# One core, attention, routed experts and a gated FFN: a spare score bank, weight splits moved to the first expert pass, and a later hand-over to the fast product

## The chip, the cores and the metric

The kernel runs on one core of a Trainium2 chip. The metric is the device time of one execution in microseconds (us). It is told as the median of the runs shown, and a profiled execution is taken beside them.

## The reference, cut to what matters

Three stages follow each other on 2304 tokens of width 512: banded causal attention, a top-2 choice among eight experts, and a gated feed-forward layer.

```python
mask = (rel >= 0) & (rel < 64)                        # attention: B=4, H=8, S=576, D=64
scores = np.where(mask, scale * q @ k.T, -1e9)
attn = softmax(scores); x = attn @ v                  # -> x [2304, 512]
logits = x @ w_gate + log1p(exp(x @ w_noise)) * noise # 8 experts, the two best are kept
for e in range(8):                                    # rows that chose e, weighted
    out[mask] += top2_w[mask, k, None] * (np.maximum(x[mask] @ w1[e], 0) @ w2[e])
h = out @ w_in                                        # 512 -> 2048
g = np.where(h >= 1, h, np.where(h <= -1, 0.0, (h + 1) ** 2 / 4))
return (g @ w_out).astype(np.float32)
```

`w_in` and `w_out` are float64 in the inputs. The kernel computes products of fp32 numbers by splitting each operand into a high part (fp32r, a copy on ScalarE) and a low part (the rest, a subtraction on VectorE), and it sums hi*hi, lo*hi and hi*lo.

## The kernel before

**Order.** The scheduler keeps the order that the program writes (`manual_schedule`), so each engine runs its instructions in that order and waits at each one for what it needs. An instruction that waits holds up all that is written behind it on the same engine.

**Attention** runs in 37 steps `step(u)`. A *unit* `u` is one score tile of 128 partitions by four heads' 128 columns. `A(i)` makes the scores of units `2i` and `2i+1` on TensorE: four mask matmuls (L352) and 32 score matmuls (L361). `top(u)` takes the maximum on VectorE (L368, L370), `soft(u)` the exponential on ScalarE (L377, four instructions), `C(u)` transposes the probabilities (L384) and copies them (L386), and `Dm(u)` multiplies with the values into the two PSUM banks `OB` (L398) and scales (L403 to L406). Scores rotate over three banks, `Sb[u % 3]`, so unit 3 uses the bank of unit 0. Before step 0 stand nine matmuls on zeros, `A(0)`, `top` and `soft` of units 0 and 1, and four more matmuls on zeros (`warm`, into `OB[:, 1, :]`). The loads of SP's queue go out in the order q and k of block 0, v of tile 0, q and k of block 1, v of tile 1.

Two other jobs ride on the steps. The routing of tokens to experts (`route`, `place`) uses VectorE for most of its small operations. The weights of the first expert come in eight chunks of 128 x 1024; of the first seven (`EW`) the high part is made by `split_w` on ScalarE and the low part by `rest_w` on VectorE (L149), one half chunk in a step; those of the sixth and seventh chunk (c = 5, 6) fall in steps 25, 26, 29 and 30.

**Experts.** `seq` is a list of (pass, chunk). Pass 0 (`0a`) takes three row blocks of expert 0, pass 1 (`0b`) the other two, pass 2 expert `e1` in six blocks, and so on to `7a` and `7b`. For a chunk `mm1` makes the hidden rows (L885), ScalarE and VectorE make their high and low parts (L893, L896) and `mm2` adds them up in one PSUM bank per block (L949). `do_mm1` runs one chunk ahead. In pass 0 `tail()`, a generator, is advanced twice per chunk; it finishes the routing (`finish_ids`, `count`). In the last chunks of a pass the rows of the next one are fetched and transposed (`xpose`: TensorE L756, ScalarE L759, VectorE L760). All six blocks of `e1` are turned in bank 7 (`TR`), and blocks 4 and 5 both at chunk 6 of pass 1 (`turn_at`).

**The gated layer.** The first group of two blocks (`g0`) runs `plain(p)` for p = 0 to 7, with two hidden chunks f = 0, 1 in each. `act_gate` makes the gate of one of them: two operations on ScalarE (L903, L904), two on VectorE (L905, L906), then the high part (ScalarE, L909) and the low part (VectorE, L910). `plain(p+1)` is written ahead of the `mm2` of p. The four groups behind it, of four blocks each, use a product with seven multiplications (`wino`, L1163). Its inputs are made out of the expert results in DRAM: the loads `prep_gather` (POOL's queue for the first such group, `g1`), `mix_two` (ScalarE L1019, VectorE L1021), the transposes `xturn` (TensorE, L1221), `xcopy` (ScalarE, L1227), the sums `xsums` (VectorE, L1240) and the splits `split_two` (ScalarE L1250, VectorE L1252). For `g1` these stand inside the plain items of `g0`. `FILL[(p, f)]` lists what `act_gate` of `plain(p)`, f does between its two VectorE operations and the high part: first the ScalarE half of each entry, and behind the low part the VectorE half. What stands under `(p, j)` is done in the seventh parts j of the `mm2` of p:

```python
FILL.update({(2, 1): [later(mix_two, units[g1], b) for b in (0, 1)],
             (3, 0): [later(mix_two, units[g1], b) for b in (2, 3)], ...
elif p == 2:
    if j in (0, 1, 5, 6):
        xturn(ui + 1, j if j < 2 else j - 3)
```

`FILL[(2, 1)]` is issued with `plain(2)`, one item ahead, so the turns of blocks 0 and 1 stand right behind `plain(3)`, at the head of the `mm2` of item 2.

Of the kernel before, what the change touches and what calls it, by code (L numbers as in the profile page):

```python
# [31 lines left out]
NB = 5  # L32
# [25 lines left out]
def fused_kernel(ctx, tc, qT, kT, v, wg, noise, wcat, out, wd=None):  # L58
# [195 lines left out]
    load_qk(0)  # L254
    load_v(0)
    load_qk(1)
# [86 lines left out]

    def A(i):
        j = i // 2
        qo, ko = (i % 2) * P, (i % 2) * P
        sb = [Sb[(2 * i + k) % 3] for k in range(2)]
        for k in range(2):
            r = slice(64 * k, 64 * k + 64)
            for c in range(2):  # L350
                m = masks[c][int((2 * i + c) % 9 == 0)]
                nc.tensor.matmul(sb[k][64 * c:64 * c + 64, :], lhsT=id64[r, :],  # L352
                                 rhs=m[r].unsqueeze(1).to_broadcast([64, 4, P]), start=True, stop=False)
        for g in range(4):
            for c in range(2):
                for k in range(2):
                    r = slice(64 * k, 64 * k + 64)
                    keys = k_t[j][r, g, ko + 64 * c:ko + 64 * c + P]
                    if c == 0:
                        keys = keys.rearrange("p (s n) -> p s n", s=2)[:, ::-1, :]  # L360
                    nc.tensor.matmul(sb[k][64 * c:64 * c + 64, g * P:g * P + P],  # L361
                                     lhsT=q_t[j][r, g, qo + 64 * c:qo + 64 * c + 64],
                                     rhs=keys, start=False, stop=(g == 3))

    def top(u):
        mx = wk.tile([P, 4], F32, tag="mx", name=f"mx{u}", bufs=3)
        nb = wk.tile([P, 4], F32, tag="nb", name=f"nb{u}", bufs=3)
        nc.vector.tensor_reduce(out=mx, in_=Sb[u % 3].rearrange("p (g n) -> p g n", g=4), axis=AX.X, op=ALU.max)  # L368

        (nc.vector if u < 4 else nc.gpsimd).tensor_scalar(out=nb, in0=mx, scalar1=-0.125, scalar2=None, op0=ALU.mult)  # L370
        mxs[u] = nb

    def soft(u):
        sb, nb = Sb[u % 3], mxs.pop(u)
        p = wk.tile([P, 4, P], F32, tag="p", name=f"p{u}", bufs=4)
        for g in range(4):
            nc.scalar.activation(p[:, g, :], sb[:, g * P:g * P + P], AF.Exp, bias=nb[:, g:g + 1], scale=0.125)  # L377
        pr[u] = p
# [294 lines left out]
    def step(u):  # L673
# [35 lines left out]
        for c in range(EW):  # L709
            for h in range(2):  # L710
                if u == L0 + LS * c + 3 + h:
                    split_w(c, h)
                if u == L0 + LS * c + 4 + h:
                    rest_w(c, slice(512 * h, 512 * h + 512))
            if u == L0 + LS * c + 4 and EW <= c + 2 < NF:
                load_raw(c + 2)
# [76 lines left out]
    def tail():  # L793
# [6 lines left out]
        count()  # L800
# [10 lines left out]
    def count():  # L811
# [25 lines left out]
                                in1=tf[:, 0:R].unsqueeze(2).to_broadcast([P, R, E]), op=ALU.is_equal)  # L837
        for a, src in enumerate((src_i, dst_i)):
# [59 lines left out]

    def act_gate(ps, hh, hl, w):
# [3 lines left out]
        nc.scalar.activation(r, ps, AF.Relu, bias=1.0)  # L903
        nc.scalar.activation(m, r, AF.Copy, scale=0.5)  # L904
        nc.vector.scalar_tensor_tensor(out=r, in0=m, scalar=1.0, in1=r, op0=ALU.min, op1=ALU.subtract)  # L905
        nc.vector.scalar_tensor_tensor(out=r, in0=m, scalar=1.0, in1=r, op0=ALU.min, op1=ALU.mult)  # L906
        for x in parts_of:
            next(x)
        nc.scalar.activation(hh, r, AF.Copy, scale=-1.0)  # L909
        nc.vector.scalar_tensor_tensor(out=hl, in0=r, scalar=-1.0, in1=hh.bitcast(F32), op0=ALU.mult, op1=ALU.subtract)  # L910
# [206 lines left out]
    def plain(ui, p):  # L1117
        w = wi[p % WS]
        for f in range(2):
# [6 lines left out]
            mm1_of(key, n, units[ui]["T"], act_gate, units[ui]["m1"], part(0), part(1))  # L1126
        load_in(p + WS)
# [130 lines left out]
    def copy_two(ui, b):  # L1258
        xcopy(ui, b)
        yield  # L1260

    def sums_two(ui, part):
        yield
        xsums(ui, part)

# [15 lines left out]
    for s in range(len(seq)):  # L1281
# [41 lines left out]
        def ahead_xpose():  # L1323
            for x, b, w in ahead:
                if f == (turn_at[b] if ui == WIDE - 1 else w + 2):
                    prep_xpose(x, b, bank[0] if ui == WIDE else TR)
# [24 lines left out]
        do_mm2(s, ahead_xpose)  # L1351
        for _ in range(SPLITS[ui][f] if ui in SPLITS else int(0 < ui < U7A)):
# [22 lines left out]
        if ui == U7B and f:  # L1375
# [6 lines left out]
          {(5, 3): (6,)})  # L1382
    g1 = FIRST2 + 1

    def later(fn, *a):
        return lambda: fn(*a)
    FILL.update({(2, 1): [later(mix_two, units[g1], b) for b in (0, 1)],
                 (3, 0): [later(mix_two, units[g1], b) for b in (2, 3)],
                 (4, 0): [later(split_two, g1, 0), later(split_two, g1, 1)],
                 (4, 1): [later(sums_two, g1, (0, 1))],  # L1390
                 (5, 0): [later(sums_two, g1, (2, 3))],
                 (5, 1): [later(split_two, g1, j) for j in (2, 3)],
                 (6, 0): [later(split_two, g1, j) for j in (4, 5)]})
    ndone = 1
    for q, (ui, p) in enumerate(items):
# [22 lines left out]
        for j in range(7):  # L1418
            if nxt:
# [12 lines left out]
                elif p == 2:  # L1432
                    if j in (0, 1, 5, 6):
                        xturn(ui + 1, j if j < 2 else j - 3)
                    for b in {3: (0, 1), 6: (2, 3)}.get(j, ()):
                        xcopy(ui + 1, b)
                for x in AT[late].get((p, j), ()):
# [40 lines left out]
```

## Time and profile before

| | |
|---|---|
| median of three runs | 971.39 us (968.99 to 973.98) |
| the profiled execution | 971.69 us, of which the span from first to last instruction is 969.9 |
| busy in the span | TensorE 944.0 us (97%), weight loads 834.8, VectorE 661.6, ScalarE 447.5, GpSimd 220.2 |
| mean granted TensorE clock | 0.994 of full speed |

TensorE is busy nearly always, so the time is that of its work, of its waits (some 26 us) and of stretches at the lower clock. A share of busy time over the whole span says little about one stage: VectorE is busy 68% of the span, and in one stretch of attention all the time.

### The profile page before, as it was taken

Reading aid. Unit: us, or ns where it says so; the run is one execution under the profiler, and the core shown is the slowest. Engines: PE = TensorE matmul, PEld = TensorE weight load, DVE = VectorE, ACT = ScalarE, POOL = GpSimd, SP = SyncE. Lnnn points to the kernel's source line nnn. Section 1 sums busy time; section 2 is a strip of 40 time slices with the busy share of each in tenths; the row PEclk is TensorE's granted clock in tenths of the full one; section 3 lists DMA queues with packets and bytes.
Section 4 is the critical chain, followed back from the end, with each engine's and each line's share of the span. In section 5 each row is a group of like instructions: output and inputs, shape, how many; then the busy total and the mean of one; then the engine's idle time right before and its main releaser. Section 6 shows DMA issues by size and latency. Waiting matters only on the chain. (4 is left out here: it accounts for less than half of the span.)

```text
span 969.9 us, 18052 instructions
## 1 busy us (share of the span) xinstructions
PE 944.0 (97%) x6781; PEld 834.8 (86%) x6781; DVE 661.6 (68%) x1388; ACT 447.5 (46%) x920; POOL 220.2 (23%) x273
## 2 busy tenths in 40 slices
PE   8998999999999999999999997999999999999998
PEld 6886878988898989889888886898999889889897
DVE  4689565378997968889543365766766677577664
ACT  6897324345555555555432355334334333443222
POOL 3221113132634354254402130013002201300000
PEclk9999999999999999999999998999999999999999
DMA  8874125445878878757727574684576558546531
GB/s 249 296 266 144 56 97 187 178 167 192 291 257 290 260 244 278 254 196 251 252 82 239 178 234 159 200 298 155 174 249 230 173 174 295 165 161 214 189 106 44
DMA packets 91274, 196.95 MB, mean 203 GB/s; under 512 B 7320, under 2 KB 18072, under 8 KB 91184
## 3 DMA queue, kind: packets, MB, share of 16 engines
q1 hardware_dynamic: 83152, 171.68, 53.6%
q0 software_dynamic: 6736, 21.86, 6.3%
q10 hardware_dynamic: 1296, 2.23, 0.6%
q8 instruction: 54, 0.88, 0.4%
q14 instruction: 36, 0.29, 0.1%
HBM read 155.45 MB, written 40.29 MB: 202 GB/s over the span
## 5 line engine op out<-in xcount | busy, mean ns | idle before, releaser
L949 PE MATMUL bank<-wo,hall 128*128 128x512 f32 x864 | 239.5, 396 | 0.0
L949 PE MATMUL bank<-w,hall 128*128 128x512 f32 (+3 forms) x944 | 236.0, 398 | 1.4 <-DVE hall L896 1.3
L949 PEld LDWEIGHTS bank<-w,hall 128*128 128x128 f32 (+3 forms) x944 | 168.4, 184 | 37.0 <-DVE hall L896 1.7
L949 PEld LDWEIGHTS bank<-wo,hall 128*128 128x128 f32 x864 | 147.8, 190 | 17.5
L893 ACT ACTIVATE hall<-bank 128x288 fp32r<-128x288 f32 (+6 forms) x128 | 54.0, 422 | 223.3 <-PE bank L885 204.1
L885 PE MATMUL bank<-xhie,w 128*128 128x288 f32 (+4 forms) x768 | 123.0, 302 | 1.6 <-DVE hall L896 1.5
L885 PEld LDWEIGHTS bank<-xhie,w 128*128 128x128 f32 x768 | 113.9, 189 | 9.1 <-DVE hall L896 3.4
L896 DVE SCALAR_TENSOR_TENSOR hall<-bank,hall 128x288 fp32r<-128x288 f32 (+7 forms) x168 | 59.8, 391 | 87.2 <-ACT hall L893 78.5
L149 DVE TENSOR_TENSOR w<-raw,w 128x1024 fp32r<-128x1024 f32 (+1 forms) x71 | 82.4, 1160 | 24.4 <-ACT w L158 20.5
L1163 PEld LDWEIGHTS bank<-xb,wi 128*128 128x128 f32 x576 | 80.4, 188 | 11.5 <-DVE wg L1148 1.2
L1187 ACT ACTIVATE hall<-cg 128x512 fp32r<-128x512 f32 x64 | 40.3, 629 | 100.5 <-DVE cg L1185 100.5
L1163 PE MATMUL bank<-xb,wi 128*128 128x256 f32 x576 | 84.8, 283 | 1.8 <-ACT r L903 0.8
L1163 PEld LDWEIGHTS bank<-xc,wi 128*128 128x128 f32 x480 | 67.2, 188 | 7.6 <-DVE wg L1148 0.6
L1030 POOL TENSOR_TENSOR y<-y,y 128x512 f32<-128x512 f32 x14 | 19.1, 1363 | 227.2 <-ACT y L1029 227.2
L1163 PE MATMUL bank<-xc,wi 128*128 128x256 f32 x480 | 70.2, 281 | 0.2
L158 ACT ACTIVATE w<-raw 128x1024 fp32r<-128x1024 f32 (+1 forms) x71 | 69.3, 976 | 0.0
L885 PE MATMUL bank<-xloe,w 128*128 128x288 f32 (+4 forms) x384 | 69.0, 301 | 0.0
L204 POOL TENSOR_TENSOR td<-rawd 128x512 f32<-128x512 f32 x32 | 33.3, 1039 | 140.7 <-DVE rawd L202 78.2
L1181 ACT ACTIVATE mg<-cg 128x512 f32<-128x512 f32 x64 | 40.1, 626 | 47.1 <-DVE cg L1153 45.4
L1182 DVE SCALAR_TENSOR_TENSOR cg<-mg,cg 128x512 f32<-128x512 f32 x64 | 47.0, 734 | 18.8 <-ACT mg L1181 18.8
L885 PEld LDWEIGHTS bank<-xloe,w 128*128 128x128 f32 x384 | 58.0, 188 | 0.0
L1191 DVE SCALAR_TENSOR_TENSOR hall<-cg,hall 128x512 fp32r<-128x512 f32 x64 | 45.9, 718 | 9.1 <-ACT hall L1187 8.7
(279 smaller groups left out, 1443.5 us busy)
## 6 DMA issues: line engine op xcount, KB each, us to landing
wi<-w1o SPq DMA_DIRECT2D x56, 1024.0 KB
raw<-wcat SPq DMA_DIRECT2D x64, 512.0 KB
rawd<-wd SPq DMA_DIRECT2D x32, 512.0 KB
w1o<-so SPq DMA_DIRECT2D x64, 256.0 KB
y<-y_dram SPq DMA_DIRECT2D x28, 256.0 KB
vE<-v SPq DMA_DIRECT2D x18, 260.0 KB
x_dram<-x SPq DMA_DIRECT2D x18, 256.0 KB
k<-kT SPq DMA_DIRECT2D x8, 512.0 KB
```

What stands on the lines that cost most here:

```text
L149: nc.vector.tensor_tensor(out=w[:, 1, c], in0=t[:, c], in1=w[:, 0, c].bitcast(F32), op=ALU.subtract)
L158: nc.scalar.activation(w[:, 0, c], t[:, c], AF.Copy)
L204: nc.gpsimd.tensor_tensor(out=t, in0=hf, in1=lf, op=ALU.add)
L885: nc.tensor.matmul(ps, lhsT=l[k], rhs=r[:, k, s:s + w], start=(c == 0), stop=(c == len(prods) - 1))
L893: nc.scalar.activation(hh, ps, AF.Relu)
L896: nc.vector.scalar_tensor_tensor(out=t, in0=ps[:, c], scalar=0.0, in1=hh[:, c].bitcast(F32), op0=ALU.max, op1=ALU.subtract)
L949: nc.tensor.matmul(M2[b][0:w], lhsT=h2[:, o:o + w], rhs=r[n], start=(first and a == 0), stop=(last and a == end))
L1163: nc.tensor.matmul(ps, lhsT=w[:, l, k * P:k * P + P], rhs=r[:, m, k, :], start=(c == 0), stop=(c == len(prods) - 1))
L1181: nc.scalar.activation(st["m"], c, AF.Relu, scale=0.5)
L1182: nc.vector.scalar_tensor_tensor(out=c, in0=st["m"], scalar=1.0, in1=c, op0=ALU.min, op1=ALU.subtract)
L1187: nc.scalar.activation(h2[:, 0:T], c, AF.Copy, scale=-1.0)
L1191: nc.vector.scalar_tensor_tensor(out=h2[:, T:2 * T], in0=c, scalar=-1.0, in1=h2[:, 0:T].bitcast(F32), op0=ALU.mult, op1=ALU.subtract)
```

## The change

1. The load of q and k of block 1 goes out ahead of v of tile 0.
2. Unit 3 takes its scores in `OB[:, 0, :]` and not in the bank of unit 0.
3. The low parts of chunks 5 and 6 are left out of the steps and made, each as one operation of 1024 columns, behind the `mm2` of chunks 0 and 2 of pass 0.
4. `count` gets a `yield` ahead of its last four operations.
5. The gate's last two operations (L909, L910) are held back to the next call of `act_gate`, behind its first one; `close_gate` does the last pair.
6. The sixth block of `e1` is transposed into bank 4, the others in bank 7 as before.
7. For `g1` the mixing, turning, copying, sums and splits move to later items.

```diff
     load_qk(0)
+    load_qk(1)
     load_v(0)
-    load_qk(1)
     load_v(1)
...
+    def score(u):
+        return OB[:, 0, :] if u == 3 else Sb[u % 3]
...
-        sb = [Sb[(2 * i + k) % 3] for k in range(2)]
+        sb = [score(2 * i + k) for k in range(2)]
...
-                if u == L0 + LS * c + 4 + h:
+                if u == L0 + LS * c + 4 + h and c < EW - 2:
                     rest_w(c, slice(512 * h, 512 * h + 512))
...
-        count()
+        yield from count()
...
+    held_gate = []
+    def close_gate():
+        for r, hh, hl in held_gate:
+            nc.scalar.activation(hh, r, AF.Copy, scale=-1.0)
+            nc.vector.scalar_tensor_tensor(out=hl, in0=r, scalar=-1.0, in1=hh.bitcast(F32), op0=ALU.mult,
+                                           op1=ALU.subtract)
+        held_gate.clear()
...
         nc.scalar.activation(r, ps, AF.Relu, bias=1.0)
+        close_gate()
         nc.scalar.activation(m, r, AF.Copy, scale=0.5)
...
+        held_gate.append((r, hh, hl))
         for x in parts_of:
             next(x)
-        nc.scalar.activation(hh, r, AF.Copy, scale=-1.0)
-        nc.vector.scalar_tensor_tensor(out=hl, in0=r, scalar=-1.0, in1=hh.bitcast(F32), op0=ALU.mult, op1=ALU.subtract)
...
+        if p == NPR - 1:
+            close_gate()
...
-                    prep_xpose(x, b, bank[0] if ui == WIDE else TR)
+                    prep_xpose(x, b, bank[0] if ui == WIDE else bank[4] if ui == WIDE - 1 and b == NB else TR)
...
         do_mm2(s, ahead_xpose)
+        if s in (0, 2):
+            rest_w(EW - 2 + s // 2, slice(0, 1024))
...
+    TURN, COPY = {(3, 0): (0,), (3, 1): (1,), (3, 6): (2,), (4, 0): (3,)}, {(3, 3): (0, 1), (4, 2): (2, 3)}
...
-    FILL.update({(2, 1): [later(mix_two, units[g1], b) for b in (0, 1)],
-                 (3, 0): [later(mix_two, units[g1], b) for b in (2, 3)],
-                 (4, 0): [later(split_two, g1, 0), later(split_two, g1, 1)],
-                 (4, 1): [later(sums_two, g1, (0, 1))],
-                 (5, 0): [later(sums_two, g1, (2, 3))],
-                 (5, 1): [later(split_two, g1, j) for j in (2, 3)],
-                 (6, 0): [later(split_two, g1, j) for j in (4, 5)]})
+    FILL.update({(3, 0): [later(mix_two, units[g1], 0)],
+                 (3, 1): [later(mix_two, units[g1], 1)],
+                 (4, 0): [later(mix_two, units[g1], b) for b in (2, 3)],
+                 (5, 0): [later(split_two, g1, j) for j in (0, 1)],
+                 (6, 0): [later(split_two, g1, j) for j in (2, 3)],
+                 (6, 1): [later(split_two, g1, j) for j in (4, 5)],
+                 (7, 0): [later(split_two, g1, 6)]})
...
+                else:
+                    for b in TURN.get((p, j), ()):
+                        xturn(ui + 1, b)
+                    for b in COPY.get((p, j), ()):
                         xcopy(ui + 1, b)
+                    if p == 4 and j > 4:
+                        xsums(ui + 1, (0, 1) if j == 5 else (2, 3))
```

## Rows read from the trace of the kernel before

**Rows 1.** Windows: stretch; busy us (count) of PE, PEld, DVE, ACT, POOL; clock; DMA share; GB/s.

```profile
30.00:40.00 10.00, 10.00 (x185) 8.96 (x188) 6.49 (x15) 9.00 (x27) 2.66 (x8) 1.00 0.81 268
...
70.00:80.00 10.00, 9.44 (x155) 8.08 (x151) 9.86 (x38) 8.78 (x27) 2.11 (x6) 1.00 0.88 297
```

**Rows 2.** Waits of TensorE over the span: who for whom, us in total, times, longest.

```profile
PE bank L1221 <- DVE y L1021: 5.5, 1, 5.5
PE bank L352 <- ACT p L377: 1.9, 2, 1.0
PE bank L756 <- DVE xloe L760: 1.8, 2, 1.5
...
PE bank L1163 <- ACT r L903: 0.8, 1, 0.8
PE bank L1163 <- ACT sg L1144: 0.6, 1, 0.6
```

**Rows 3.** Timeline of the start: start, duration, instruction [idle before, releaser].

```profile
7.94 2.17 ACT L377 ACTIVATE p<-bank,nb 128x128 f32<-128x128 f32 x8 [5.86 <-DVE nb L370]
9.13 0.41 PE L352 MATMUL bank<-mask,id 64*64 64x512 bf16 x2 [0.95 <-ACT p L377]
10.97 0.40 POOL L114 COPY k<-k 128x256 f32<-128x256 f32 x1 [1.42 <-DMA k<-kT]
11.03 0.60 ACT L386 ACTIVATE pt<-bank 128x512 f32<-128x512 f32 x1 [0.92 <-PE bank L384]
12.71 0.40 PE L352 MATMUL bank<-mask,id 64*64 64x512 bf16 x2 [0.94 <-ACT p L377]
```

**Rows 4.** The low parts in attention: group over 69 to 95 us, then VectorE's timeline.

```profile
L149 DVE TENSOR_TENSOR w<-raw,w x4: 681/682/689, 70.6 to 88.1; 128x512 fp32r<-128x512 f32 x4
...
70.64 0.69 DVE L149 TENSOR_TENSOR w<-raw,w 128x512 fp32r<-128x512 f32 x1
71.24 0.69 DVE L368 TENSOR_REDUCE mx<-bank 128x4 f32<-128x512 f32 x1
```

**Rows 5.** Windows of attention's late steps, same columns as rows 1.

```profile
69.00:96.50 27.50, 23.71 (x390) 19.52 (x382) 26.56 (x111) 21.27 (x65) 4.37 (x13) 1.00 0.49 163
```

**Rows 6.** Timeline of pass 0 where the routing goes on.

```profile
116.08 0.56 DVE L896 SCALAR_TENSOR_TENSOR hall<-bank,hall 128x384 fp32r<-128x384 f32 x1 [0.47 <-ACT hall L893]
117.05 0.21 DVE L540 TENSOR_TENSOR ohs<-o 128x48 bf16<-128x48 f32 x1
117.45 0.20 PE L555 MATMUL bank<-ohs,tri 128*128 128x48 bf16 x1
117.64 1.22 DVE L149 TENSOR_TENSOR w<-raw,w 128x1024 fp32r<-128x1024 f32 x1
```

**Rows 7.** Windows between TensorE's instructions around its two longest waits, columns as in rows 1.

```profile
140.00:142.00 2.00, 0.73 (x3) 0.29 (x3) 1.97 (x5) 0.79 (x2) 0.95 (x1) 1.00 0.94 305
...
167.17:174.49 7.32, 5.86 (x29) 5.10 (x27) 2.93 (x5) 2.20 (x4) 0.00 (x0) 0.77 0.37 121
174.49:176.41 1.92, 1.92 (x13) 1.92 (x13) 0.52 (x1) 0.46 (x1) 0.00 (x0) 1.00 0.23 92
...
576.00:578.74 2.74, 2.74 (x14) 2.25 (x13) 1.58 (x4) 1.72 (x6) 2.74 (x5) 1.00 0.83 249
578.74:581.73 2.99, 2.99 (x25) 2.78 (x23) 0.98 (x3) 0.51 (x2) 0.40 (x1) 1.00 1.02 370
581.73:594.48 12.75, 7.22 (x30) 6.03 (x29) 5.45 (x11) 7.07 (x15) 0.00 (x0) 0.73 0.50 188
```

**Rows 8.** TensorE's timeline in a later group: four transposes and what follows.

```profile
653.98 0.60 PE L1221 MATMUL bank<-idn,y 128*128 128x128 f32 x4
654.33 0.96 PE L1163 MATMUL bank<-xb,wi 128*128 128x256 f32 x6
```

**Rows 9.** The timelines of ScalarE and VectorE where the mixed rows arrive.

```profile
585.06 0.72 ACT L1019 ACTIVATE y<-y,wts 128x512 f32<-128x512 f32 x1 [2.73 <-DMA y<-y_dram]
...
586.46 0.75 DVE L1021 SCALAR_TENSOR_TENSOR y<-y,wts 128x512 f32<-128x512 f32 x1
```

More of the change, by code (lines that the diff above doesn't have):

```diff
@@ L367, in top @@
         nb = wk.tile([P, 4], F32, tag="nb", name=f"nb{u}", bufs=3)
-        nc.vector.tensor_reduce(out=mx, in_=Sb[u % 3].rearrange("p (g n) -> p g n", g=4), axis=AX.X, op=ALU.max)
+        nc.vector.tensor_reduce(out=mx, in_=score(u).rearrange("p (g n) -> p g n", g=4), axis=AX.X, op=ALU.max)
         (nc.vector if u < 4 else nc.gpsimd).tensor_scalar(out=nb, in0=mx, scalar1=-0.125, scalar2=None, op0=ALU.mult)
@@ L373, in soft @@
     def soft(u):
-        sb, nb = Sb[u % 3], mxs.pop(u)
+        sb, nb = score(u), mxs.pop(u)
         p = wk.tile([P, 4, P], F32, tag="p", name=f"p{u}", bufs=4)
@@ L837, in count @@
                                 in1=tf[:, 0:R].unsqueeze(2).to_broadcast([P, R, E]), op=ALU.is_equal)
+        yield
         for a, src in enumerate((src_i, dst_i)):
@@ L1256, in xsplit @@
             pass
[L1258 to L1264, printed above, removed]
     SPLITS = {0: [int(F0 <= f < F0 + NF - EW) for f in range(NF)], 1: [0] + [1] * (NF - 1),
@@ L1381, in fused_kernel @@
     AT = ({(4, 0): (None,), (4, 4): (0,), (4, 5): (1,), (5, 0): (2,), (5, 1): (3,), (5, 3): (4,), (6, 2): (5,), (6, 3): (6,)},
-          {(5, 3): (6,)})
+          {})
+    TURN, COPY = {(3, 0): (0,), (3, 1): (1,), (3, 6): (2,), (4, 0): (3,)}, {(3, 3): (0, 1), (4, 2): (2, 3)}
     g1 = FIRST2 + 1
@@ L1431, in fused_kernel @@
                         xcopy(ui + 1, 2 * (p - 2) + j // 2)
[L1432 to L1435, printed above, removed]
+                else:
+                    for b in TURN.get((p, j), ()):
+                        xturn(ui + 1, b)
+                    for b in COPY.get((p, j), ()):
                         xcopy(ui + 1, b)
+                    if p == 4 and j > 4:
+                        xsums(ui + 1, (0, 1) if j == 5 else (2, 3))
                 for x in AT[late].get((p, j), ()):
```

## The prediction

> **What bounds the kernel now.** I read the windows of the span first, then who waited for whom on TensorE, and then the timelines around each wait that the change touches. TensorE is the bound almost everywhere: in the steady part of attention it has no idle time at all [rows 1]. So only what shortens its waits, or its time at the lower clock, counts. The list of waits has one large entry, 5.5 us at the first transposes for `g1`, and a handful of 1 to 2 us [rows 2]. Two further things are not in that list. In attention's late steps VectorE is busy 26.56 of 27.50 us while TensorE is busy 23.71, so there VectorE sets the pace and TensorE waits in small pieces for it [rows 1, 5]. And in the stretches behind two of the waits the granted clock is 0.77 and 0.73 [rows 7]: the clock has only two levels, so part of that work ran at 1.2 GHz.
>
> **Load order and score bank.** `A(1)` needs the bank that `soft(0)` still reads, and TensorE waits 0.95 us for it; a second wait, of 0.94 us, is for the bank of unit 2, which `soft(2)` reads [rows 3]. With unit 3 in `OB`, `A(1)` runs right behind the warm-up matmuls. ScalarE, which idles 0.92 us between the first eight exponentials (7.94 + 2.17 = 10.11) and the copy at 11.03 [rows 3], gets its next work that much sooner; from there on it is nearly busy, so the chain moves by that idle time, and `soft(2)` and the second wait with it, rather than by both waits. I take 1.0 us; ends 0 (the second halves of q and k of block 0, whose landing no row shows, come no sooner) and 1.9 (both waits gone). The steps behind are bound by TensorE, so the gain isn't lost on the way [rows 1]. The load order is its cover: a copy waits for k of block 1 until 10.97 [rows 3], q of that block is issued behind it, and `A(2)` would now want both at about 11. The two loads of v that now stand behind are first used by `Dm(1)`, two steps later.
>
> The Trainium skill (DMA: Bandwidth & Descriptors, Queues, rings and completion order) says that each DMA engine consumes a queue's descriptors in ring order. By it the new order lets k and q of block 1 land sooner and v of tile 0 later, so the term would be 1.0 if v is still in time for `Dm(1)` and nearer to 0 if not, which the ends above hold. The trace agrees as far as it goes: k of block 1, seventh in the queue, is what its copy waits for; it shows no wait for v there.
>
> **Low parts out of attention.** Four operations of 0.68 us [rows 4] leave the stretch in which VectorE is the bound. They follow each other into the next operation in 0.60 us (70.64 to 71.24 [rows 4]), so VectorE's chain shortens by 4 x 0.60 = 2.4 us. TensorE idles 27.50 - 23.71 = 3.79 us there [rows 5], so it can follow. Value -2.4; ends -2.4 and 0 (if the waits are latencies of a chain and not VectorE's load).
>
> They come back as two operations of 1.22 us [rows 6] in pass 0. The first is queued ahead of the chain that makes `ohs`: the low part L896 that VectorE waits 0.47 us for, then the routing's operations up to 117.26 (117.05 + 0.21), while TensorE starts on `ohs` at 117.45 [rows 6]. Slack 0.47 + 0.19 = 0.66, so 1.22 - 0.66 = 0.6 us of wait is new. The second stands ahead of a batch of marks, whose users come a whole `mm1` later; I put 0.1 for it. Value +0.7; ends 0 and +2.4 (both in full). Behind the marks TensorE waits for `place`, and with it pass 0.
>
> **`count`.** Its second half is now issued one advance later, yet still ahead of the next `mm1`, so VectorE's order stays as it was: 0. What covers it is that nothing stands between the two advances on VectorE; POOL's next fetch only moves behind one that it is not waiting for.
>
> **Bank 4.** The sixth transposes of `e1` wait for VectorE to empty bank 7: the 1.5 us in the list [rows 2]. From the fifth transposes to the second hidden chunk of `e1` are 7.32 us at a mean clock of 0.77 [rows 7]. At the full clock that stretch holds twelve matmuls of 1.92 us together (the next window), six of L949, which are half of 2.74 [rows 7], and two groups of transposes of 0.35 us each (653.98 to 654.33 [rows 8]): 1.92 + 1.37 + 0.70 = 3.99. So 7.32 - 3.99 = 3.3 us go if the wait goes and the clock stays. Value -3.3; ends -1.5 (the wait alone) and -3.4. Bank 4 is free there, since pass 0 used it last and has been evicted.
>
> **The later hand-over.** In the old order the turn of block 0 stands behind `plain(3)`, and the mix of block 1, queued on ScalarE and VectorE ahead of block 0's result, waits for a load from DRAM until 585.06 [rows 9]; TensorE reaches the turn at about 581.7. The stretch from there to `plain(4)` is 12.75 us at a clock of 0.73, for work that takes 2.74 (twelve L949) plus 16 transposes, 4 x 0.35: 4.14 us [rows 7, 8]. In the new order the `mm2` of item 2 has nothing in front of it and `plain(4)` follows: 581.73 + 2.74 + 2.99 = 587.5 before the first turn, by which time block 1 (585.06 + 0.72 + 0.75 = 586.5 [rows 9]) is mixed and block 0 long since. Gain 12.75 - 4.14 = 8.6, the 16 transposes being paid later. Value -8.6; ends -5.5 (the wait alone) and -8.6. Late next is `plain(4)`'s gate: its first ScalarE operation is queued behind the mix of block 1, ends its wait at 585.8 and finds its matmuls just done. The next banks and hidden rows are wanted later still, so 1 to 2 us of lateness stay hidden.
>
> **The gate held back.** It moves each pair of operations behind the next chunk's first one, so that PSUM banks come free sooner; the hidden rows come one chunk later but are wanted by an `mm2` that stands a whole item behind. Both waits where the fast product begins are for such an operation: 0.8 for the last gate's first operation (L903, removed) and 0.6 for a copy behind its last (L1144) [rows 2]. The second can grow, since sums and splits now crowd into VectorE's last items. Value -0.4; ends -1.4 (both go) and +1.7 (the second grows to 1.5 and the clock falls as at bank 4, where the loss beyond the wait is 3.3 - 1.5 = 1.8, less a little).
>
> **Sum.** -1.0 - 2.4 + 0.7 - 3.3 - 8.6 - 0.4 = -15.0, against the profiled execution's 971.7: **956.7 us**. That execution lies 0.3 above the median of the runs.
>
> **Rivals.**
> - *The clock falls elsewhere.* A wait of 1.27 us at 140 to 142 kept the clock at 1.00, the one of 1.5 us at bank 4 was followed by the low level [rows 2, 7]; the new wait where the fast product begins lies between. Price 1.7: 958.4.
> - *VectorE gives its gain back.* TensorE's small waits in attention also come from chains of dependent operations, and pass 0 takes the low parts in full: 0.9 instead of 2.4, +2.4 instead of +0.7: 956.7 + 1.5 + 1.7 = 959.9. Against it: VectorE's near-solid row.
> - *The rows from DRAM come later,* because the loads of gate weights no longer wait and share the DMA engines, whose share is 1.02 in that window [rows 7]; ScalarE then holds the gates up. Half of 8.6 back: 961.0.
> - *The waits go but the clock does not come back:* 3.1 of 8.6 and 1.8 of 3.3 lost: 961.6.
> - *The hand-over doesn't do what it says:* the turn still waits in some other queue: 965.3.
> - *Slower.* ScalarE is in order, and the mix of block 1 now stands ahead of the gates of `plain(4)`. Each microsecond by which block 1 lands after about 587 is one on TensorE; to be 5 us over the old time it would have to land some 20 us later, at 607. Nothing in the rows points to that: about 976.6.
>
> **How the numbers follow.** Chances: forecast 0.60, clock elsewhere 0.12, VectorE 0.12, late rows 0.08, clock lost 0.03, no hand-over 0.03, slower 0.02. About half a per cent, 4.9 us, is what a measurement can tell here from no change. The terms' good ends give 971.7 - 1.9 - 2.4 - 3.4 - 8.6 - 1.4 = 954.0, and the bad ends, which won't meet, 968.8. The range 954 to 962 holds the first five cases and leaves out the last two and what is unforeseen. Faster (under 966.5) are the first six cases, less a little for the unforeseen: 0.94; the same 0.04; slower 0.02.
>
> **What would show it.** No wait of L1221 above 1 us and a clock of 1.00 from 570 to 600; no wait of L756 for L760 above 0.5 and 1.00 around the change to `e1`; the first `mm1` about 3.4 us sooner than before; a new wait of L555 of about 0.6; a wait at the third product of `wino` of 0.5 to 1.5. The prediction is wrong if ScalarE's mix of block 1 ends after 588 on the times of the kernel before, if L631 waits as before, or if the low clock shows up in a new place.

## The result and the profile after

The changed kernel takes **955.48 us** (median of 5 runs, 954.46 to 956.81) against 971.39 us for the kernel before (median of 5, 968.99 to 973.98): ratio **0.9838**, 95% interval 0.9819 to 0.9857. Its profiled execution has a span of 953.8 us, 16.1 less than before, and a mean granted clock of 1.000 (0.994 before). Run again later, beside other kernels (e9 below), it took 956.18 us against 969.23 (ratio 0.9866, 0.9849 to 0.9883): there the gain is 13.05 us, here 15.91.

The waits of TensorE in the changed kernel, the list that answers to [rows 2]:

```profile
PE bank L889 <- DVE hall L900: 1.5, 3, 1.1
PE bank L962 <- DVE hall L900: 1.3, 1, 1.3
PE bank L659 <- DVE wz L95: 1.2, 1, 1.2
PE bank L634 <- DVE ohe L593: 0.9, 5, 0.3
PE bank L1178 <- ACT sg L1159: 0.9, 1, 0.9
```

Lines have moved: L756 is now L759, L949 L962, L885 L889, L896 L900, L1163 L1178, L1221 L1236, L1019 and L1021 (the mixes) L1032 and L1034; the gate's L903 is L916, its copy L909 and low part L910 are L907 and L908. In e8 and e10 they stand up to three lines further down. The two entries that the change was costed by, 5.5 us at L1221 and 1.8 us at L756 for VectorE, are gone from the head of the list. Where they stood TensorE is busy throughout, at the full clock. Windows of the changed kernel, columns as in [rows 1], to be held against [rows 7]:

```profile
140.00:165.00 25.00, 25.00 (x171) 22.75 (x170) 14.43 (x24) 12.33 (x23) 9.33 (x8) 1.00 0.60 193
165.00:180.00 15.00, 15.00 (x85) 13.93 (x84) 6.72 (x11) 4.82 (x8) 4.73 (x4) 1.00 0.72 256
560.00:580.00 20.00, 20.00 (x135) 18.24 (x134) 13.26 (x29) 11.44 (x28) 6.34 (x8) 1.00 0.88 304
580.00:600.00 20.00, 20.00 (x137) 18.36 (x137) 15.66 (x34) 13.23 (x34) 0.00 (x0) 1.00 0.55 177
```

And attention's late steps, to be held against [rows 5]; TensorE's busy time in a window of the same length is up by 1.71 us:

```profile
68.00:95.50 27.50, 25.42 (x432) 21.50 (x424) 25.22 (x110) 22.05 (x66) 6.36 (x14) 1.00 0.53 168
```

Where the time came from is read by one method in all runs: the start of the same matmul in two traces, at places where a stretch ends. The table gives how much later each starts than in the changed kernel's first profile (us; the first row is that profile's own clock). "Attention" is early in its steady part, "in pass 1" between pass 0 and the turning of `e1`, "past bank 4" after the first chunks of `e1`, "third" the third product of `wino`.

| kernel | attention | first `mm1` | in pass 1 | past bank 4 | `plain(1)` | `plain(7)` | third | last `mm2` |
|---|---|---|---|---|---|---|---|---|
| *changed, at us* | 39.15 | 103.08 | 152.19 | 178.35 | 560.45 | 595.75 | 601.81 | 949.40 |
| before | 0.92 | 3.81 | 3.52 | 7.18 | 6.79 | 15.37 | 16.12 | 16.17 |
| e1 old hand-over | 0.04 | -0.24 | -0.23 | -0.23 | -0.13 | 4.35 | 4.32 | 4.34 |
| e2 bank 7 | 0.35 | 0.08 | 0.09 | 3.20 | 3.24 | 3.24 | 3.24 | 3.30 |
| e3 bank 7, filled | 0.15 | -0.22 | -0.19 | 1.34 | 0.86 | 0.87 | 0.87 | 0.92 |
| e4 low parts back | 0.29 | 2.35 | 2.09 | 2.09 | 1.81 | 1.81 | 1.82 | 1.84 |
| e5 three banks | 1.10 | 1.78 | 1.83 | 2.20 | 2.77 | 2.75 | 2.76 | 2.79 |
| e6 old load order | 2.12 | 2.76 | 2.77 | 3.26 | 3.46 | 3.46 | 3.47 | 3.48 |
| e7 gate not held | 0.26 | 0.93 | 0.98 | 1.42 | 1.69 | 2.00 | 4.37 | 4.92 |
| e8 count later | 0.30 | 0.95 | -0.08 | 0.37 | 1.06 | 1.04 | 1.04 | 1.06 |
| e9 changed, again | 0.33 | -0.08 | -0.07 | -0.07 | 0.26 | 0.24 | 0.24 | 0.28 |
| e10 both waits | 0.24 | 1.19 | 1.34 | 1.38 | 2.50 | 2.51 | 1.43 | 1.35 |
| e11 hand-over and gate old | 0.15 | 0.46 | 0.42 | 0.46 | -0.03 | 6.72 | 7.48 | 7.52 |
| e12 mixes old | -0.15 | 0.24 | 0.28 | 0.28 | 1.18 | 3.52 | 3.52 | 3.62 |

So the change's gain, read down the row of the kernel before: 0.9 at the start, 2.9 to the first `mm1`, 0.3 lost in pass 0, 3.7 at bank 4, 0.4 given back over 380 us, 8.6 at the hand-over, 0.75 from there to the third product.

### The profile page after: what moved, and what is told of

It reads as the page before. It is cut to its first block, busy times and chain, and to the rows that moved or that the text cites. A ratio compares the mean times of both kernels' runs of the same rounds, so it can differ in the third digit from the quotient of the medians.

```text
span 953.8 us, 18052 instructions
## 1 busy us (share of the span) xinstructions
PE 939.1 (98%) x6781; PEld 831.4 (87%) x6781; DVE 660.2 (69%) x1386; ACT 444.7 (47%) x920; POOL 219.9 (23%) x273
## 5 line engine op out<-in xcount | busy, mean ns | idle before, releaser
L962 PE MATMUL bank<-wo,hall 128*128 128x512 f32 x864 | 237.6, 394 | 0.0
L962 PE MATMUL bank<-w,hall 128*128 128x512 f32 (+3 forms) x944 | 234.9, 396 | 1.4 <-DVE hall L900 1.3
L962 PEld LDWEIGHTS bank<-w,hall 128*128 128x128 f32 (+3 forms) x944 | 167.7, 183 | 36.8 <-DVE hall L900 1.7
L962 PEld LDWEIGHTS bank<-wo,hall 128*128 128x128 f32 x864 | 146.7, 188 | 17.4 <-DVE hall L908 0.2
L889 PE MATMUL bank<-xhie,w 128*128 128x288 f32 (+4 forms) x768 | 122.6, 302 | 1.6 <-DVE hall L900 1.5
L889 PEld LDWEIGHTS bank<-xhie,w 128*128 128x128 f32 x768 | 113.4, 188 | 9.0 <-DVE hall L900 3.5
L900 DVE SCALAR_TENSOR_TENSOR hall<-bank,hall 128x288 fp32r<-128x288 f32 (+7 forms) x168 | 59.7, 391 | 83.8 <-ACT hall L897 83.7
L1178 PEld LDWEIGHTS bank<-xb,wi 128*128 128x128 f32 x576 | 80.5, 188 | 10.7 <-ACT sg L1159 1.4
L1178 PE MATMUL bank<-xb,wi 128*128 128x256 f32 x576 | 84.7, 282 | 1.2 <-ACT sg L1159 0.9
L1178 PEld LDWEIGHTS bank<-xc,wi 128*128 128x128 f32 x480 | 67.2, 188 | 7.6 <-DVE wg L1163 0.6
L1178 PE MATMUL bank<-xc,wi 128*128 128x256 f32 x480 | 70.2, 281 | 0.2
L889 PE MATMUL bank<-xloe,w 128*128 128x288 f32 (+4 forms) x384 | 69.0, 301 | 0.0
L889 PEld LDWEIGHTS bank<-xloe,w 128*128 128x128 f32 x384 | 58.0, 188 | 0.0
```

Of the source, the lines that this page charges most:

```text
L889: nc.tensor.matmul(ps, lhsT=l[k], rhs=r[:, k, s:s + w], start=(c == 0), stop=(c == len(prods) - 1))
L900: nc.vector.scalar_tensor_tensor(out=t, in0=ps[:, c], scalar=0.0, in1=hh[:, c].bitcast(F32), op0=ALU.max, op1=ALU.subtract)
L962: nc.tensor.matmul(M2[b][0:w], lhsT=h2[:, o:o + w], rhs=r[n], start=(first and a == 0), stop=(last and a == end))
L1178: nc.tensor.matmul(ps, lhsT=w[:, l, k * P:k * P + P], rhs=r[:, m, k, :], start=(c == 0), stop=(c == len(prods) - 1))
```

## The experiments

Each kernel is the changed one with one edit (e10 and e11 with two, e9 with none). They were run in three groups, each on one chip: e1 to e4, e5 to e8, e9 to e12. What an edit costs is read where its stage lies, since stages far from it move by up to 1.1 us from one execution to the next (in e10's row 1.38 to 2.50 between the first chunks of `e1` and `plain(1)`, where nothing was edited).

**e1, the hand-over's old places** (fills, turns, copies and splits; the gate stays held):

```
-    FILL.update({(3, 0): [later(mix_two, units[g1], 0)],
-                 (3, 1): [later(mix_two, units[g1], 1)],
-                 (4, 0): [later(mix_two, units[g1], b) for b in (2, 3)],
...
+    FILL.update({(2, 1): [later(mix_two, units[g1], b) for b in (0, 1)],
+                 (3, 0): [later(mix_two, units[g1], b) for b in (2, 3)],
...
+                elif p == 2:
+                    if j in (0, 1, 5, 6):
+                        xturn(ui + 1, j if j < 2 else j - 3)
```

> The changed kernel with the fills, turns, copies and splits of the seventh unit's hand-over at their old places; everything else as changed. Theory (the hand-over is worth 8.6 us): plain(7) starts about 8.6 us later against wino's first product, the time is near 964; a PE wait of over 4 us for the ACT mix at the low-part line comes back, and the granted clock falls under 0.8 in the 10 to 14 us behind it. Rival (the wait moves with the rest of the change and is hidden by now): under 2 us, near 956, clock 1.00 throughout.

Measured 959.45 us. From `plain(1)` to `plain(7)` it loses 4.48 us, half of what the theory says, though the wait and the low clock do come back. TensorE's timeline of e1:

```profile
576.04 0.66 PE L1236 MATMUL bank<-idn,y 128*128 128x128 f32 x4 [1.55 <-DVE y L1034]
...
578.00 1.11 PE L1236 MATMUL bank<-idn,y 128*128 128x128 f32 x4 [1.07 <-DVE y L1034]
```

and the window behind them:

```profile
577.79:585.00 7.21, 7.00 (x38) 6.17 (x39) 3.76 (x9) 4.78 (x11) 0.00 (x0) 0.77 0.42 156
```

There are two waits of 1.55 and 1.07 us in place of one of 5.5 [rows 2]. So part of the 8.6 is due to another edit; e7 and e11 look for it.

**e7, the gate not held:**

```
         nc.scalar.activation(r, ps, AF.Relu, bias=1.0)
-        close_gate()
...
         for x in parts_of:
             next(x)
+        close_gate()
         for x in parts_of:
             next(x, None)
```

> The changed kernel with the last part of the gate's chain in the plain stage made at its old place, behind the other parts, rather than held until after the next block's first step. Theory (the 0.75 us between plain(7) and wino's third product is this edit's): 0.75 us, near 956.2; two PE waits of 0.8 and 0.6 us at the low-weight lines come back in place of the one of 0.9. Rival (the 0.75 us is due to the hand-over's other timing): under 0.2 us, near 955.5.

Measured 960.60 us. The edit costs 3.2 us (1.69 at `plain(1)`, 4.92 at the end), four times the theory's price; 2.4 of it lie between `plain(7)` and the third product (2.00 to 4.37). In e7's timelines ScalarE's copy of the hidden rows (L907) stands in front of the next chunk's first operation (L916) and waits for VectorE, which the sums and splits now fill; TensorE's wait, at the second product, comes behind it:

```profile
603.14 0.42 ACT L907 ACTIVATE hall<-r 128x256 fp32r<-128x256 f32 x1 [1.25 <-DVE r L919]
603.46 0.36 ACT L916 ACTIVATE r<-bank 128x256 f32<-128x256 f32 x1
...
603.88 1.65 PE L1178 MATMUL bank<-xb,wi 128*128 128x256 f32 x6 [1.69 <-ACT r L916]
```

The window of e7 behind that wait:

```profile
603.88:607.50 3.62, 3.62 (x14) 3.09 (x15) 2.25 (x6) 1.08 (x3) 0.00 (x0) 0.53 0.40 153
```

**e11, the hand-over of e1 and the gate of e7 together:**

> The changed kernel with the hand-over's places of e1 and the gate's chain of e7 both as before the change. Theory (each of the two edits alone covers part of the same lateness: with ScalarE standing at the mix for a transfer, a gate that isn't held is late as well): the start of plain(7)'s first product comes 8.3 to 8.9 us later than in the changed kernel, and wino's third product 9.0 to 9.7, more than e1 (4.4) and e7 (0.3 and 3.2) add up to. Rival (the two are independent): 4.4 to 4.9 at plain(7), 7.4 to 7.8 at wino's third product.

Measured 963.86 us: 6.75 us from `plain(1)` to `plain(7)`, 7.5 to the third product and to the end. e1 and e7 add up to 4.5 + 3.2 = 7.7. In size the rival is right, the two edits add; in place neither is, and that makes the agreement in size chance: with the old places the gate's share is 2.3 us at the hand-over (6.75 less 4.48) and 0.8 behind it, with the new places 0.3 and 2.4. Why the gate counts at the hand-over is seen in VectorE's and, below the dots, TensorE's timeline of e11,

```profile
578.64 0.43 DVE L908 SCALAR_TENSOR_TENSOR hall<-r,hall 128x256 fp32r<-128x256 f32 x1 [5.41 <-ACT hall L907]
578.98 1.41 DVE L1034 SCALAR_TENSOR_TENSOR y<-y,wts 128x512 f32<-128x512 f32 x2
...
579.78 1.12 PE L1236 MATMUL bank<-idn,y 128*128 128x128 f32 x4 [4.87 <-DVE y L1034]
```

against VectorE's of e1:

```profile
575.23 0.75 DVE L1034 SCALAR_TENSOR_TENSOR y<-y,wts 128x512 f32<-128x512 f32 x1 [4.05 <-ACT y L1032]
577.19 0.75 DVE L1034 SCALAR_TENSOR_TENSOR y<-y,wts 128x512 f32<-128x512 f32 x1 [1.21 <-ACT y L1032]
```

With the gate not held, VectorE's low part L908 waits for the copy L907, which ScalarE makes behind the mix of block 1, and block 0's result stands behind L908. With the gate held nothing lies between, and block 0 is turned when its own mix is done. That is nearly the old wait (4.87 of 5.53 us), and the held gate alone halves it, to the 1.55 and 1.07 us of e1.

**e12, only the four mixes at their old places,** transposes and splits left where the change put them:

> The changed kernel with the four mixes of the seventh unit at their old places (one to three fills earlier); transposes, copies, sums and splits stay where the change put them, and the gate is held. Theory (what costs in e1 is where the transposes stand in PE's queue, and ScalarE's early stand at the mix is covered by the held gate): under 0.5 us, no PE wait over 0.5 at the transposes. Rival (the early mix itself, which holds ScalarE for the gathered rows, is what costs): 2 to 4.4 us, with a PE wait of 1 us or more in the stage, at mm2 for the hidden values or at the transposes.

Measured 958.62 us; the theory fell and the rival held. 2.34 us are lost between `plain(1)` and `plain(7)`, and TensorE waits at `mm2`. The timelines of ScalarE and TensorE in e12:

```profile
576.40 0.72 ACT L1032 ACTIVATE y<-y,wts 128x512 f32<-128x512 f32 x1 [4.82 <-DMA y<-y_dram]
577.81 0.72 ACT L1032 ACTIVATE y<-y,wts 128x512 f32<-128x512 f32 x1 [0.69 <-DMA y<-y_dram]
578.70 0.41 ACT L907 ACTIVATE hall<-r 128x256 fp32r<-128x256 f32 x1
...
579.16 1.74 PE L962 MATMUL bank<-wo,hall 128*128 128x512 f32 x6 [1.93 <-ACT hall L907]
```

The window of e12 behind it:

```profile
579.16:583.00 3.84, 3.84 (x26) 3.42 (x27) 3.05 (x8) 2.97 (x7) 0.00 (x0) 1.00 0.77 289
```

ScalarE stands 4.82 us at a mix for the gathered rows, and the hidden rows queued behind it reach `mm2` late. In the changed kernel's timeline the same mixes wait 0.26 and 0.71 us:

```profile
574.51 0.73 ACT L1032 ACTIVATE y<-y,wts 128x512 f32<-128x512 f32 x1 [0.26 <-DMA y<-y_dram]
...
576.84 0.72 ACT L1032 ACTIVATE y<-y,wts 128x512 f32<-128x512 f32 x1 [0.71 <-DMA y<-y_dram]
```

Counted from the start of `plain(1)`, the mix of a block starts within 1.7 us of the same time in the kernel before, the changed one, e1, e11 and e12, so the rows come about when they did; the change asks for them later. Both moves count: the mixes out of ScalarE's way (2.3 here), the transposes out of TensorE's (with both moved back, e1, it is 4.5).

**e2, the sixth transposes in bank 7 again, and e3, the same with six idle matmuls ahead of them** (they write a free bank and feed nothing):

```
-                    prep_xpose(x, b, bank[0] if ui == WIDE else bank[4] if ui == WIDE - 1 and b == NB else TR)
+                    if ui == WIDE - 1 and b == NB:
+                        for _ in range(6):
+                            nc.tensor.matmul(bank[4], lhsT=idr, rhs=whi[n], start=True, stop=True)
+                    prep_xpose(x, b, bank[0] if ui == WIDE else TR)
```

> The changed kernel with the sixth early transpose block of the fourth unit back in the transpose bank that the fifth uses. Theory (wait and clock together are the bank's 3.6 us): near 959.1; a PE wait of 1.3 to 1.5 us at the transposes, and behind it some 3 us of PE work at a granted clock near 0.77. Rival (only the wait is the bank's, the low clock had another cause): 1.5 us, near 957, clock 1.00 behind the wait.

> As e2, but with six matmuls of 512 columns that write a free bank and feed nothing, put between the fifth and the sixth transposes, so that PE has work while it would wait; this work is extra. Theory (the clock falls because PE stands still): the clock stays at 1.00 there, PE waits under 0.3 us, and the cost against the changed kernel is that of the six matmuls alone, 1.3 to 2.0 us (near 957). Rival (the clock falls for another cause, such as the small transposes themselves): the cost is that of e2 or more, 3.6 us and up, with the granted clock near 0.77 behind it.

e2 measured 958.23 us, e3 957.33. At its place e2 costs 3.1 us (0.09 to 3.20), e3 1.5 (-0.19 to 1.34). TensorE's timeline of e2:

```profile
165.12 0.50 PE L759 MATMUL bank<-idr,xge 64*128 64x64 f32 x4 [1.46 <-DVE xloe L763]
```

with the window behind it,

```profile
165.12:168.50 3.38, 3.38 (x13) 2.87 (x14) 1.65 (x2) 1.33 (x2) 0.00 (x0) 0.65 0.33 126
```

and the timeline of e3, where the idle matmuls are L1335,

```profile
163.21 1.62 PE L1335 MATMUL bank<-w,idr 128*128 128x512 f32 x6
164.83 0.50 PE L759 MATMUL bank<-idr,xge 64*128 64x64 f32 x4
```

with its window:

```profile
165.26:168.50 3.24, 3.24 (x18) 2.98 (x18) 1.65 (x2) 1.33 (x2) 0.00 (x0) 1.00 0.18 72
```

Both theories hold: the wait and the low clock behind it make up the bank's price, and work that is of no use saves the second half (3.1 less 1.5, 1.6 us in the traces; 0.9 between the medians, e3's profile being the fastest of its four runs). The new bank is better still, since it needs neither.

**e4, the low parts back in attention:**

```
-                if u == L0 + LS * c + 4 + h and c < EW - 2:
+                if u == L0 + LS * c + 4 + h:
...
-        if s in (0, 2):
-            rest_w(EW - 2 + s // 2, slice(0, 1024))
```

> The changed kernel with the low parts of the sixth and seventh early weight chunks made in the attention steps again. Theory (the low parts are the cause of the attention's gain of 2.9 us, and cost 0.3 us in the first expert pass): first mm1 2.9 us later, pass 0 shorter by 0.3, near 958.1. Rival (0.5 us of the 2.9 is a late signal of that one execution and not the low parts' doing): first mm1 2.4 us later, near 957.6. A second rival (the start's own gain runs on, and the low parts are hidden): under 1 us, near 956.

Measured 958.29 us. The first `mm1` comes 2.35 us later than in the changed kernel's profile and 2.3 to 2.6 later than in e1 to e3, its neighbours; pass 0 is 0.26 shorter: 2.1 in all. The first rival was right: some 0.5 of the 2.9 us read between the two profiles is not the low parts'. The kernel before waits at a transpose late in attention (L419, now L422), and e4, which has the low parts back, doesn't:

```profile
99.93 0.66 PE L419 MATMUL bank<-idn,x 128*128 128x128 f32 x4 [0.82 <-DVE x L406]
```

e5 to e8 wait there too (below). What brings this wait in some executions stays open.

**e5, three score banks, and e6, the old load order:**

```
 def score(u):
-        return OB[:, 0, :] if u == 3 else Sb[u % 3]
+        return Sb[u % 3]
```

```
-    load_qk(1)
     load_v(0)
+    load_qk(1)
```

> The changed kernel with the fourth score block in the three-bank rotation again; the new load order is kept. Theory (the start's 0.95 us is the bank's): the attention steps begin 0.95 us later, near 956.4, with a PE wait of about 0.9 us at the scores for the ACT exponentials. Rival (the gain is the load order's): under 0.2 us, near 955.5.

> The changed kernel with the first head's loads in the old order (values ahead of the second head's queries and keys); the fourth bank for the scores is kept. Theory (bank and order work together: the score block in the fourth bank needs the later loads sooner): the steps begin 0.3 to 0.6 us later, near 956. Rival (the loads are there in time either way): 0, near 955.5.

e5 measured 958.74 us, e6 957.82. At 39 us e5 is 1.10 late and e6 2.12, where the two other kernels of their group are 0.26 and 0.30. The waits of e5, then of e6:

```profile
PE bank L355 <- ACT p L380: 1.9, 2, 0.9
...
PE bank L364 <- DMA qbuf<-qT: 1.2, 2, 0.8
```

```profile
PE bank L364 <- DMA qbuf<-qT: 2.0, 3, 0.8
```

In e5 the second wait for the exponentials is back, as its theory says, and so is ScalarE's idle time ahead of its first copy (L389, L386 before), which the prediction went by. ScalarE in e5, then in the changed kernel:

```profile
10.54 0.60 ACT L389 ACTIVATE pt<-bank 128x512 f32<-128x512 f32 x1 [0.92 <-PE bank L387]
```

```profile
10.00 0.65 ACT L389 ACTIVATE pt<-bank 128x512 f32<-128x512 f32 x1
```

From the first exponential to that copy are 3.09 us in e5 (from 7.45) and before, 2.01 in the changed kernel (from 7.99). But e5's first exponential came 0.54 us sooner, so the net price is less.

In e6 TensorE waits for queries instead, 2.0 us in three places, which is more than either theory allowed for. None of the three need be the load order's. The first, 0.85 us, is `A(1)`'s, for the second half of q of block 0, which goes out ahead of v in both orders; e9 and e10, with the new order, wait there 0.78 and 1.01 us. At the second (0.42 us, `A(2)`) e1 waits 0.41, at the third (0.69, near 32 us) e5 waits 0.44. And e6's profile was the longest of its four runs (957.32 to 958.96). So that the order is the bank's cover is not shown, and the price of each alone, at most 0.8 us for the bank and 1.8 for the order at 39 us, isn't settled.

**e8, the second half of the count one step later; e10, that and the last held gate made behind the second fast product;** two waits left in the changed kernel (1.28 us at L962, 0.92 at L1178):

```
-        yield from count()
+        c = count()
+        next(c)
+        yield
+        for b in range(1, units[1]["nb"]):
+            prep_gather(units[1], b)
+        yield
+        next(c, None)
...
-        if p == NPR - 1:
-            close_gate()
...
             for x in then[j]:
                 x(ps)
+            if j == 1:
+                close_gate()
```

> The changed kernel with the second half of the token count (and the two weight loads behind it) one step later, so that VectorE makes the gate product of the first expert pass's seventh chunk ahead of it. Theory (PE's wait of 1.28 us at mm2 of that chunk is for VectorE, which is held by the count): the wait falls under 0.3 us and the time by 1.0 to 1.3, near 954.3. Rival (the count or the loads behind it are late then, and PE waits as long a step later): 0, near 955.5, or up to 1 us slower.

> The changed kernel with two moves: the second half of the token count one step later, as in e8, and the last held part of the gate made behind the second Winograd product rather than ahead of the first. Theory: the first wait of 1.28 us goes but for 0.3 (as in e8), and ScalarE copies the first Winograd product out before it waits for VectorE, so that the wait of 0.92 us at the third product falls under 0.2: 1.7 to 2.0 us under the changed kernel of the same call. Rival: VectorE's sums of the second product are what PE waits for next, and half of the 0.92 comes back: 1.2 to 1.5 us under.

> The changed kernel, nothing altered: what chip and execution alone do to the starts by which the other runs are compared. If the 0.9 us at the late attention and the two 0.45 us later on, which four kernels with unrelated edits had in common, belong to the execution and not to the edits, this run shows them too or shows neither: 955.5 to 957.5. If it stays at 955.5 without them in the same company in which the next kernel has them, they are the edits' own.

e8 measured 956.25 us, e10 **954.38** (953.73 to 956.84), the changed kernel beside it (e9) 956.18 (955.45 to 957.22). In both, pass 0 is 1.0 us shorter at the wait's place (in e10 from 2.35 late ahead of it to 1.34 behind it): the 1.28 go, and half a microsecond is lost again at a low part, 0.27 of it as a wait. In e10 the product's wait is gone too, 2.51 to 1.43. (e10's profile is the slowest of its five runs. It is late at pass 0 because the clock was low there, as the window shows.) TensorE in e8, then ScalarE in e10, where the copy of the first product (L1160) now precedes the last hidden rows (L910):

```profile
140.68 0.74 PE L892 MATMUL bank<-xlo0b,w 128*128 128x256 f32 x4 [0.27 <-DVE xlo0b L763]
```

```profile
602.48 0.37 ACT L1160 ACTIVATE sg<-bank 128x256 f32<-128x256 f32 x1
603.58 0.42 ACT L910 ACTIVATE hall<-r 128x256 fp32r<-128x256 f32 x1 [0.74 <-DVE r L923]
```

and the window at the start of pass 0 in e10:

```profile
103.20:106.50 3.30, 3.30 (x10) 2.51 (x9) 0.69 (x1) 0.60 (x1) 0.00 (x0) 0.50 0.00 0
```

The two terms come to 2.1 in the trace and 1.8 in the medians, which is within what the theory gave, though 1.8 us are less than what a measurement of this kernel can tell safely; the waits in the traces are the better evidence. e10 is the fastest version that was run.

e9 answers its own question: e5 to e8 have 0.9 us in common at the late attention and twice some 0.4 later, e9 has none of it. In all four the first of these is a TensorE wait that the trace puts down to nothing but issue (a stretch in which it waited for nothing that the profile shows), here in e8:

```profile
97.09 0.66 PE L422 MATMUL bank<-idn,x 128*128 128x128 f32 x4 [0.88 <-issue]
```

e10 contains e8's edit and has none of the three either. Those steps are the executions', not the edits'.

e9 also shows, in the changed kernel itself, the unfavourable end that the prediction gave the start: `A(1)` waits 0.78 us for the second half of q of block 0, and ScalarE idles 0.59 us of the old 0.92 again.

## Why the prediction was right

956.7 was forecast, 955.48 came, and the sum of -15.0 stands against -16.1 in the two profiles. Term by term:

- **Start, -1.0:** -0.9 between the profiles. e5 shows the mechanism, the idle 0.92 us of ScalarE, with a smaller net price. What the load order does isn't shown: no list of waits read here has one for v, and e6's waits for q are met without the old order too.
- **Attention, -2.4:** right. e4 gives 2.35 us (the 2.9 between the profiles holds some 0.5 of another kind), so VectorE's chain was the bound there, and the operations' start-to-start time was the price.
- **Pass 0, +0.7:** mis-sized, +0.26 by e4. The new wait of 0.6 at L555 (now L558) didn't come; L558 starts 0.29 us late (113.93 against 117.45 less the 3.81 by which pass 0 begins sooner). The first low part ran ahead of the maxima and of the hidden rows' low part (VectorE's timeline below); it held up what is behind it by 1.0 us rather than 1.22, and L900 was only 0.44 late, since half of that fell into the 0.47 us for which VectorE idled there before [rows 6]. The VectorE rival fell with it. The last line is TensorE's.

```profile
110.36 1.22 DVE L149 TENSOR_TENSOR w<-raw,w 128x1024 fp32r<-128x1024 f32 x1
111.49 0.51 DVE L530 MAX8 mx<-ny 128x8 f32<-128x8 f32 x6
...
112.71 0.56 DVE L900 SCALAR_TENSOR_TENSOR hall<-bank,hall 128x384 fp32r<-128x384 f32 x1
...
113.93 0.18 PE L558 MATMUL bank<-ohs,tri 128*128 128x48 bf16 x1
```

- **Bank 4, -3.3:** right; 3.7 between the profiles, 3.1 by e2, of which 1.6 is the clock's by e3.
- **Count, 0:** right for the change (nothing moved), but the count's place was not free: e8 gained 1.0 us by moving it further.
- **Hand-over, -8.6, and gate, -0.4: the sum held between the profiles (9.3 us) and the division was wrong.** This is the step that failed. The prediction put the whole 12.75 us stretch down to the places of mixes and turns and gave the gate only the waits at the fast product. The runs give 4.5 for the places and 3.2 for the gate. The gate's edit takes VectorE's low part, and with it ScalarE's stand at block 1, out of block 0's way. Without it, and with the sums and splits moved late, the wait for the last gate's first operation, 0.8 us before and by the prediction removed, grows to 1.69 us with a low clock behind it (e7). The prediction's bad end (+1.7) is a wait and a low clock of that size, but at the other wait, the third product's, and as a danger with the gate held rather than as what the gate prevents.
- What is left, 9.3 in the profiles against 7.5 in e11, is 1.8 us, and the trace says where it lies. In that stretch the kernel before waits 5.53 us, e11 4.87 (counted from `plain(1)`, block 1's mix starts 0.66 us later in the kernel before), and in the 7.22 us behind it the granted clock is 0.61, in e11 0.78: 0.66 + 7.22 x 0.17 = 1.9. That this belongs to the one execution that was costed, and not to the edits in which e11 still differs from the kernel before, is likely but not shown. Windows of before, then of e11:

```profile
587.26:594.48 7.22, 7.21 (x29) 6.03 (x29) 4.31 (x9) 4.29 (x10) 0.00 (x0) 0.61 0.10 36
```

```profile
579.78:587.00 7.22, 7.22 (x39) 6.36 (x40) 4.30 (x9) 4.55 (x10) 0.00 (x0) 0.78 0.17 62
```

Whole runs point the same way: the kernel before, run 23 times beside the experiments, took 967.6 to 969.2 us in the six runs with a mean clock of 0.998, 968.2 to 970.9 in the twelve at 0.996, and 969.8 to 974.6 in the five at 0.995 or less. The profile that was costed, 971.69 us, has 0.994. Nine runs of the changed kernel lie between 954.5 and 957.2. So a change that removes such a stall also removes its spread, and a single profile prices it only to a microsecond or two.

Added up from the runs that undo them, the terms come to -0.9 - 2.35 + 0.26 - 3.1 - 7.5 = -13.6, near the 13.05 us of the second measurement. So -15.0 is more than the change is worth against a typical run of the kernel before. The forecast was close all the same, because the 971.7 from which it is taken and the stalls that it takes off are of one execution, whose longer stall stands in both.

Of the rivals none came: the clock is at 1.00 behind the new wait at the third product (0.92 us, ahead of 601.81, window of the changed kernel below), the rows landed in time, and the mix of block 1 ended at 578.3, well before its turn at 580.7.

```profile
601.81:605.00 3.19, 3.19 (x23) 3.02 (x24) 1.37 (x5) 0.00 (x0) 0.00 (x0) 1.00 0.51 196
```

## What to carry to other kernels

When an engine works its queue in order, the price of a late transfer is that of everything queued behind the instruction that waits for it, on that engine and on the next one; look for every edit that takes something out from behind it before giving the whole stall to one. Terms that act on the same stall should be costed together and divided only by runs that undo them singly and jointly. Where TensorE must stand for a microsecond or two, matmuls that feed nothing can cost less than the low clock behind the wait (1.5 us against 3.1 here), but another bank is cheaper still.

## What was not expected of the hardware

The length of a TensorE wait did not tell whether the clock would fall. A wait of 1.93 us (e12) and one of 1.28 us (L962 in the changed kernel) were followed by 1.00; one of 1.46 us (e2) by a mean of 0.65 over 3.4 us, one of 1.69 us (e7) by 0.53 over 3.6 us; in e1 the clock was at 0.98 after the first wait of 1.55 us and at 0.77 after a second of 1.07 us close behind it; and in e10 waits of only 0.45 and 0.56 us, 1.9 us apart at the end of attention, were followed by 0.50 over 3.3 us, while 0.45 and 0.41 us at the same places in e11 were followed by 1.00. The window of the changed kernel right behind its wait of 1.28 us:

```profile
138.20:141.50 3.30, 3.30 (x20) 3.00 (x21) 1.61 (x3) 0.00 (x0) 0.00 (x0) 1.00 0.98 381
```

What tells the cases apart stays open; e3 shows only that without a wait it stayed up. The Trainium skill (TensorE: Matmul & The Clock Gate, Loop structure matters more than you think) has VectorE's copying of a result out of PSUM as something that doesn't break TensorE's warmth, in a loop whose next matmuls follow immediately. Here they didn't follow immediately, TensorE waited for such a reading of a bank, and both outcomes came: behind the 1.28 us (L962 for L900) the clock stayed at 1.00, behind the 1.46 us of e2 (L759 for L763) it was low.
